# Sums and denominators of seven attention slabs by one operation of eight products, realigned through DRAM; first loads and operation order changed

## The chip, the core and the metric

The kernel runs on one core of a Trainium2 chip. A core has five engines that run side by side, each through its own list of instructions in order: PE (matrix products; its weight loads are listed apart as PEld), DVE and ACT (elementwise work and reductions on up to 128 partitions), POOL (the same, slower) and SP (which here only issues DMAs). ACT can issue DMAs too. DMAs move data between DRAM and the core's memory (SBUF); products land in PSUM, eight banks of 128 partitions x 512 FP32 values, from where DVE or ACT copy them out. Engines wait for each other by semaphores. The metric is the device time of one execution in microseconds (us), as a median over runs.

## The reference

Four blocks in a row on x (2048 tokens, 512 features): attention, gated MLP, attention, gated MLP, each on a layer-normalised copy and added to x. The attention is linear, with 32 heads of 16 features:

```python
pq = jnp.einsum("bhsd,hdf->bhsf", q, w_phi)
pk = jnp.einsum("bhsd,hdf->bhsf", k, w_phi)
phi_q = jnp.concatenate([_softmax(pq, axis=-1), _softmax(-pq, axis=-1)], axis=-1)
phi_k = jnp.concatenate([_softmax(pk, axis=-1), _softmax(-pk, axis=-1)], axis=-1)
kv = jnp.einsum("bhsf,bhsd->bhfd", phi_k, v)
z  = jnp.einsum("bhsf->bhf", phi_k)
num = jnp.einsum("bhqf,bhfd->bhqd", phi_q, kv)
den = jnp.einsum("bhqf,bhf->bhq", phi_q, z)[..., None] + 1e-6
o = num / den
```

The MLP is `h = relu(x @ W_gate) * (x @ W_up)`, `h @ W_down`, with 1376 hidden features. Both layers use the same weights.

What matters for the change: for every query and head the softmaxes of pq and -pq need two sums of exponentials (sign 0 and sign 1, 16 terms each), and den needs two more products, exponentials times z. From these four numbers the kernel makes one factor for each sign, so that it can multiply the bare exponentials instead of dividing three times: with sums Z0, Z1 and denominators D0, D1, the factor of sign s is Z(1-s) / (D0 Z1 + D1 Z0).

## The kernel before, in words

The 16 tiles of 128 tokens stand in five slabs of 2, 4, 4, 4 and 2 tiles (`SLABS`), 256 or 512 tokens each. x stays in SBUF. For each layer the program goes through these stages; the tag in brackets is the one in the code, followed by layer and slab:

- layernorm to a normalised, transposed copy (`la`, and `lg` ahead of the MLP). It is transposed either by a DMA on SP's queue (L848, for the keys in `XPOSE`) or by PE in strips of 32 (L872) with four copies. Slab 2 of layer 0 (`a02`) is done by PE.
- keys (`k`): k and v products, exponentials of both signs (L900), their sums (L906) and reciprocals, v scaled by them (L920), products into `kvsum` (L932, L942). All slabs must be through before the sums stage `su` can use `kvsum`.
- queries (`q`): products into a bank, exponentials of both signs into `expq` (L1001).
- `attend`: sums of exponentials (`z`, with the stationary block `ZO`) and denominators (`at`, with `ZD`), both at L1016. A slab has 32 + 32 small products: for each of four column strips (32 columns of the array) a quarter of the slab's tokens, so that the results lie as (quarter, head) on 128 partitions. ACT copies the sums out (`Zs`, L1050), DVE multiplies (`zm`, L1058) and adds (`zden`, L1060), ACT takes the reciprocal by Ln and Exp (L1061, L1062), DVE makes the factors `aT` (L1063).
- spreading (`sp`): the factors must reach the 16 rows of every head. Slabs 0 and 1 do that by PE (L1137) with DVE and ACT behind it; slabs 2, 3 and 4 by DRAM: two writes (L1073) and eight broadcast reads (L1077) on SP's queue into `abT` (four chunks, one for eight heads), then one product for each chunk on DVE or POOL (L1122).
- numerators (`nm`, L1089, 32 products on 16 tiles of 32 x 32), output projection (`wo`), residual (L1159).
- MLP (`gx` and `gl` for gate and up, `d` for down); slab st + 1's attention is put into the program ahead of slab st's MLP.

The order on each engine is fixed when the program is built. A planner (`Program.schedule`) walks through all operations with estimated durations and takes, at each step, the ready operation that can start first; the list `TURNS`, one number for each operation, decides among them. The table `ENG` says which engine takes an eviction, a scaling or a load. On the chip each engine then follows its list and waits where its semaphores tell it to; a wait on SP's queue holds every DMA behind it.

The plain products of all stages go through `mm` (L673); `evict` (L769 to L775) copies a bank out by DVE or ACT.

The branch that the change switches on is in the code already (L1025 to L1039), but `ZALL = ()`:

```python
if (L, st) in ZALL:
    def all_sums(e):
        for s in range(2):
            for c in range(NC):
                ins = e.matmul(zd.f32()[32 * c:32 * c + 32, 0:n], ZA[:, s, c, :], eqv(st)[:, c, s, :], start=s == 0, stop=s == 1, tile_position=(0, 32 * c))
        return ins
```

Of the kernel before, what the change touches and what calls it, by code (L numbers as in the profile page):

```python
# [12 lines left out]
P = 128  # L13
# [10 lines left out]
ENG = {'ap/a00/0': 'act',  # L24
 'ap/a01/3': 'dve',
 'ap/a02/2': 'dve',
 'ap/a02/3': 'dve',
# [3 lines left out]
 'ap/a11/0': 'act',  # L31
 'ap/a11/3': 'act',
 'ap/a12/1': 'act',
 'ap/a12/2': 'act',
 'ap/a12/3': 'act',
 'ap/a13/1': 'act',
 'ap/g01/1': 'act',
 'ap/g01/2': 'act',
 'ap/g01/3': 'act',
 'ap/g02/0': 'act',  # L40
 'ap/g03/1': 'act',
 'ap/g03/2': 'act',
 'ap/g03/3': 'act',
 'ap/g04/0': 'act',
 'ap/g04/1': 'act',
 'ap/g11/1': 'act',
 'ap/g11/3': 'act',
 'ap/g12/3': 'act',
 'ap/g13/2': 'act',
 'ap/g13/3': 'act',  # L50
 'ap/g14/0': 'act',
 'ap/g14/1': 'act',
 'em/00/01': 'dve',
 'em/01/01': 'dve',
 'em/10/01': 'dve',
 'em/10/03': 'dve',
 'em/11/03': 'dve',
 'es/02/1': 'pool',
 'es/02/2': 'pool',
 'es/02/3': 'pool',  # L60
# [3 lines left out]
 'es/04/3': 'pool',  # L64
 'es/12/1': 'pool',
# [4 lines left out]
 'es/14/0': 'pool',  # L70
 'es/14/2': 'pool',
 'fcq0': 'dve',
 'fcq2': 'dve',
 'ld/wk2': 'sp',
 'ld/x1': 'act',
 'ot/00/3': 'act',
 'ot/01/1': 'dve',
 'ot/01/3': 'dve',
 'ot/02/1': 'dve',
 'ot/02/3': 'dve',  # L80
 'ot/03/1': 'dve',
 'ot/04/2': 'dve',
 'ot/10/0': 'dve',
 'ot/10/2': 'dve',
 'ot/10/3': 'act',
 'ot/11/1': 'dve',
 'ot/12/0': 'dve',
 'ot/12/2': 'dve',
 'ot/13/3': 'dve',
 'ot/14/2': 'dve',  # L90
 'rz/0/12': 'act',
 'rz/0/13': 'act',
 'rz/0/14': 'act',
 'rz/0/4': 'act',
 'rz/0/6': 'act',
 'rz/0/9': 'act',
 'rz/1/11': 'act',
 'rz/1/12': 'act',
 'rz/1/14': 'act',
 'rz/1/15': 'act',  # L100
 'rz/1/3': 'act',
 'rz/1/4': 'act',
 'rz/1/5': 'act',
 'rz/1/8': 'act',
 'vc/0/13': 'dve',
 'vc/0/3': 'dve',
 'vc/0/6': 'dve',
 'vc/0/7': 'dve',
 'vc/1/1': 'dve',
 'vc/1/11': 'dve',  # L110
 'vc/1/12': 'dve',
 'vc/1/2': 'dve',
 'vc/1/3': 'dve',
 'vc/1/5': 'dve',
 'vc/1/6': 'dve',
 'vc/1/8': 'dve',
 'vh/0/10/1': 'dve',
 'vh/0/12/1': 'dve',
 'vh/0/13/1': 'dve',
 'vh/0/14/0': 'dve',  # L120
 'vh/0/15/0': 'dve',
 'vh/0/15/1': 'dve',
 'vh/0/6/1': 'dve',
 'vh/0/8/0': 'dve',
 'vh/0/8/1': 'dve',
 'vh/1/0/0': 'dve',
 'vh/1/1/0': 'dve',
 'vh/1/10/0': 'dve',
 'vh/1/11/0': 'dve',
 'vh/1/12/0': 'dve',  # L130
# [3 lines left out]
 'vh/1/2/0': 'dve',  # L134
# [4 lines left out]
 'vh/1/7/0': 'dve',  # L139
 'vh/1/8/0': 'dve',  # L140
 'vh/1/9/0': 'dve',
 'vh/1/9/1': 'dve',
 'xp/a02': 'pe',
# [3 lines left out]
 'yc/a00/1': 'dve',  # L147
 'yc/a01/00': 'act',
 'yc/a01/03': 'act',
 'yc/a02/02': 'act',  # L150
 'yc/a03/00': 'act',
# [20 lines left out]
 'yc/g11/03': 'act',  # L172
# [3 lines left out]
 'yc/g14/03': 'act'}  # L176
XPOSE = ('a02', 'a03', 'a04', 'a11', 'a12', 'a13', 'g01', 'g02', 'g03', 'g12', 'g13', 'g04', 'g14')
XISSUE = 1270.0
XDELAY = 215.0
BIG = 'sp'  # L180
# [3 lines left out]
ZALL = ()  # L184
TURNS = """
-28 300 427 180 240 186 0 614 40 120 554 928 1235 801 988 674 1362 1422 1115 1175 1482 1602 1662 1782 1542 1722 56 6 0 84 174 104 211 54 124 64 144 76
119 161 204 247 290 332 375 91 76 117 191 242 218 696 181 629 635 640 646 680 726 732 737 743 805 801 806 812 818 886 845 850 856 861 903 778 784 790
795 838 867 873 878 884 1009 241 357 386 424 542 570 663 668 674 680 728 299 373 405 440 252 318 560 566 571 771 980 1002 1023 1090 1306 1327 1366
1387 1141 1237 1318 1484 1477 1550 1656 959 1045 1067 1112 1219 1241 1263 1284 1189 1381 1598 1772 1429 1943 1837 1923 2201 2737 1794 1842 1848 1908
1955 1349 1355 1360 1539 1573 1653 1702 1854 1859 1895 1609 1615 1642 1647 1733 36 549 48 534 638 756 580 764 793 828 896 963 1002 934 1003 1072 970  # L190
1165 1333 1250 1284 1285 1729 1750 1799 1821 1772 2019 2062 2084 2092 1906 2287 2529 2237 2594 2700 1431 1452 1517 1659 1409 1544 1620 1680 1858 1800
2014 2187 1814 2252 2358 1474 1495 1566 1587 1865 1976 1997 2105 1685 1637 2629 2776 2808 2189 2953 2847 2329 2394 2416 2437 1707 1886 1954 2040 2535
2487 2794 2962 2140 3165 3059 2868 3304 3441 838 1243 1069 1526 1185 1533 1127 1706 1781 1848 1881 1888 1954 2023 2122 2155 2232 2462 2428 2495 2395
2643 2664 2772 2815 2600 2621 2686 2708 2870 2918 3004 3246 3310 2902 3349 3741 2729 2751 2949 2971 3100 3187 3208 3230 3069 3021 3177 3384 3324 3561
3455 3014 3036 3057 3079 3122 3144 3165 3273 3262 3129 3476 3692 3327 3906 3843 2794 2837 2928 2992 3364 3429 3450 3472 3444 3511 3584 3790 3993 3559
4137 4031 3892 4328 4505 2229 2779 1426 1874 1714 2787 1540 2772 2825 2860 3112 3317 3177 3375 3804 3285 3270 3524 3856 3397 3537 3559 3580 3602 3623
3645 3688 3710 3732 3684 3969 4095 3876 4243 4349 3839 3952 3973 4016 4038 4060 4081 4103 4066 4114 4187 4355 4162 4455 4561 4124 4146 4168 4189 4211
4232 4431 4517 4287 4239 4397 4602 4667 4619 4705 4818 3775 3818 3861 3995 3667 3731 3753 3796 4410 4506 4579 4734 4799 4295 4944 4881 4700 5235 5352
3119 3426 3492 3626 3734 3807 3983 2571 3433 3607 3780 3836 3924 4110 4254 4276 4297 4388 4582 4604 4647 4668 4554 4458 4687 4819 4884 4751 5163 5050
4409 4452 4539 4770 4474 4496 4560 4625 4836 4900 4973 5099 4686 5226 5289 5285 5412 5465 5515 5559 5525 2589 4759 4868 4998 5117 5150 5182 5215 5363  # L200
5315 3493 3504 3515 3526 4857 4901 4912 4987 5027 5075 5474 5531 5605 5662 5697 5751 5783 5821 5875 5998 6092 5939 5949 6058 6384 6456 6476 6486 6516
6550 6572 6593 6748 6812 6926 7073 6615 6636 6726 6769 6791 6868 6977 7011 7044 7121 7208 7272 7278 7284 7289 7326 6984 7025 7063 7095 7185 7191 7196
7202 7273 2127 2148 2170 2308 2358 2406 2567 3252 3385 3407 3636 4009 2459 2481 2502 2524 2632 2583 2286 2351 2373 2545 2680 2728 4801 4948 5630 5725
5773 5813 5850 5893 6232 6543 6304 6383 6340 6602 6090 6151 6147 6509 6244 6196 6443 6668 6749 6808 6797 6749 7295 7316 7338 7360 7419 6990 7033 7208
7251 7595 6925 7055 7076 7098 7148 6947 6968 7012 7229 7360 7537 7771 7713 7793 7655 7786 7479 7778 7822 7895 7941 7927 7934 8111 8093 7955 8024 8302
8429 8048 8175 7414 7597 7616 7625 7917 7947 8097 8138 8210 8278 8676 7381 7392 7477 7488 7532 7542 7586 7633 7786 7797 8117 8127 8147 8158 8168 8179
7672 8219 7422 7433 7444 7564 7575 7753 7764 7808 7403 7709 7840 7873 7895 7906 7925 7936 7847 7975 7499 7666 7687 7698 7731 7742 7829 7884 7955 7966
8010 8021 8032 8065 8223 8234 8348 8431 7510 7521 7553 7644 7655 7775 7851 8054 7676 7819 7862 8075 8086 8106 8201 8212 8300 8372 7455 7466 7605 7720
7977 7988 7999 8043 8190 8245 8256 8267 8278 8289 8343 8805 8162 8845 8321 8354 8375 8397 8551 8573 8594 8616 8927 8949 9357 9407 8300 8419 8440 8462
8646 8676 8697 8719 8971 8992 9039 9089 9587 9706 9175 9249 9735 9809 9893 9921 10033 10068 10255 13237 13259 13269 13340 14966 14988 15096 15290  # L210
13392 13441 13519 13682 15390 15624 15463 15074 15441 15873 15916 12933 13019 13062 13154 15966 16014 16107 16287 13198 16347 16410 19480 19501 19560
5052 5074 5096 5128 5219 5267 4944 5161 5381 5509 5559 5607 4879 4966 5009 5031 5123 5171 4923 5193 5338 5359 5411 5459 5733 5871 6002 6211 6363 6436
6594 6636 6751 6691 7087 7207 7327 7267 7027 6907 6967 7147 7827 7887 7389 7603 8493 8622 8633 8574 8574 9601 9688 9709 10076 10126 9753 9904 10012
10163 10259 8762 8784 8816 8838 8904 9731 9796 9817 9839 9900 10201 10319 10334 10408 8979 9053 9975 10099 10438 10473 10505 10558 10557 10621 10589
10991 10610 10864 10737 9298 9306 9487 9495 9504 9555 9563 9571 9608 9714 8638 8667 8903 8911 8919 9014 9022 9030 9067 9148 9881 9276 9422 9465 9925
10184 10271 10292 10379 9990 10429 9512 9623 9645 9666 9082 9444 9533 9580 9761 9833 8859 9190 9211 9233 9168 9255 9314 9401 9283 9467 9947 10098
10120 10228 10249 10314 10336 10400 10510 10654 10530 10552 10573 10595 9860 9882 9968 9990 10645 10717 8741 8881 9060 9103 10638 10660 10681 10703
9548 10776 10357 10444 10465 10487 10141 10422 10508 10616 10734 10836 9125 9147 9336 9379 11159 11246 11289 11375 10798 11425 9774 10033 10055 10206
10987 11051 11073 11138 10857 11188 10724 10746 10789 10832 10767 10811 10854 10875 10917 11047 12184 12205 12227 12249 12270 12317 12363 12385 12436
# [133 lines left out]
class Program:  # L353
    SYNC = 120.0
    SAME = 60.0
    DMA_ISSUE = {"sp": 600.0, "act": 560.0, "pool": 1100.0}
    DMA_LAT = 1800.0
    DMA_BW = 270.0
    SWITCH = 95.0
# [64 lines left out]
    def schedule(self):  # L424
# [6 lines left out]
        qfree = ported = 0.0  # L431
# [897 lines left out]
```

## Time and profile before

| | us |
|---|---|
| median of 3 runs | 390.58 (389.74 to 391.33) |
| the profiled execution | 390.76 |
| its span, first to last instruction | 389.0 |
| PE busy | 373.5 (96% of the span) |
| DVE, ACT, POOL busy | 275.5, 193.8, 66.6 |
| sums and denominators, 640 products at L1016 | 10.7 (sum of their busy times) |
| DMA moved | 24.33 MB, most of it in the first 30 us |

Busy time of an engine is the time in which it works on an instruction; a matmul is listed with its whole passage through the array (379 ns for 512 columns), although the next one starts 0.22 us behind it, so that the busy time of PE overlaps and says little about how dense the work is. The chain of waits goes back from the last instruction to what released each step; its pieces give the true pace of consecutive products. In the table of groups a line is one kind of instruction at one line of the code, with its count, its total and mean time, and the idle time ahead of it on its engine. The code's lines (L...) are those of the kernel before.

### The profile page before, as it was taken

The page shows a single profiled execution, that of the slowest core. Times are in us where ns is not written, and L with a number is a line of the kernel's source. Part 1 is how long each engine was busy: PE and PEld are TensorE (multiplying, and loading weights), DVE is VectorE, ACT ScalarE, POOL GpSimd, SP SyncE. Part 2 cuts the span into 40 slices and gives each one's busy share as a digit, 9 for nine tenths or more (in the row PEclk, how much of TensorE's full clock was granted, in tenths as well). Part 3 has the DMA queues.
Part 4 walks back from the last instruction along what each step waited for, and adds up shares of the span by engine and source line. Part 5 has one row for each costly group of instructions (what it writes and reads, how often), then busy time and mean ns, then how long its engine had stood idle before and what let it go on. Part 6 is the DMA issues. An engine that isn't in the chain of part 4 may idle for free.

```text
span 389.0 us, 9735 instructions
## 1 busy us (share of the span) xinstructions
PE 373.5 (96%) x4097; PEld 201.7 (52%) x4151; DVE 275.5 (71%) x561; ACT 193.8 (50%) x432; POOL 66.6 (17%) x59
## 2 busy tenths in 40 slices
PE   6999998999999999999999999999999999999996
PEld 3555455584444444454456555558444454444574
DVE  8999988885973676994359997899778234344343
ACT  4899899562360334393135659975153213212320
POOL 0168440151310000121003124003530000000000
PEclk9999999999999999999999999999999999999999
DMA  9992200224340000431000200015540201010111
GB/s 211 297 357 46 48 3 3 90 72 112 109 68 2 13 0 15 95 56 40 0 3 17 48 16 17 4 60 133 133 108 15 45 11 41 27 29 28 42 34 54
DMA packets 53067, 24.33 MB, mean 63 GB/s; under 512 B 38976, under 2 KB 52000, under 8 KB 53024
## 3 DMA queue, kind: packets, MB, share of 16 engines
q1 hardware_dynamic: 52208, 23.51, 24.2%
q8 instruction: 32, 0.52, 0.6%
q10 hardware_dynamic: 816, 0.21, 0.3%
q14 instruction: 11, 0.09, 0.1%
HBM read 12.89 MB, written 2.42 MB: 39 GB/s over the span
## 4 chain that ended last, share of the span: by engine, by line
PE 85%; ACT 4%; DMA 3%; DVE 3%; issue 2%; SPq 1%
PE pb L673 80%; DMA yG<-ytile 2%; ACT expk L900 2%; PE pb L932 2%; PE pb L1016 1%; DMA x_sb<-in_A_x_dram 1%; DVE expq L1155 1%; PE pb L1089 1%; SPq L848 1%; ACT expq L1001 1%; DVE stats L798 0%; ACT gate_sb L1211 0%; ACT ytile L840 0%; DVE oT L771 0%; PE pb L872 0%
## 5 line engine op out<-in xcount | busy, mean ns | idle before, releaser
L673 PE MATMUL pb<-yG,Wg 128*128 128x512 bf16 (+1 forms) x394 | 100.3, 336 | 1.1 <-DMA yG<-ytile 0.7
L673 PE MATMUL pb<-yG,Wu 128*128 128x512 bf16 (+1 forms) x393 | 98.6, 336 | 0.6 <-issue 0.3
L1211 ACT ACTIVATE gate_sb<-pb 128x512 bf16<-128x512 f32 x80 | 47.1, 596 | 104.3 <-PE pb L673 81.5
L673 PE MATMUL pb<-Wd,hT 128*128 128x512 bf16 (+2 forms) x352 | 97.1, 373 | 1.5 <-issue 0.9
L1213 DVE TENSOR_TENSOR hT<-gate_sb,pb 128x512 bf16<-128x512 bf16 x80 | 53.7, 683 | 53.9 <-PE pb L673 39.2
L920 POOL TENSOR_TENSOR vhat<-vsb,rZk 128x544 bf16<-128x544 bf16 x38 | 41.1, 1101 | 140.9 <-DVE x_sb L1159 48.1
L1159 DVE TENSOR_TENSOR x_sb<-x_sb,pb 128x512 bf16<-128x512 bf16 x59 | 39.4, 679 | 29.3 <-PE pb L673 28.9
L673 PEld LDWEIGHTS pb<-yG,Wg 128*128 128x128 bf16 x400 | 39.0, 98 | 31.2 <-issue 1.0
L673 PEld LDWEIGHTS pb<-yG,Wu 128*128 128x128 bf16 x400 | 38.9, 98 | 30.4 <-DVE hT L1213 0.2
L673 PEld LDWEIGHTS pb<-Wd,hT 128*128 128x128 bf16 (+1 forms) x363 | 35.0, 98 | 35.6 <-issue 2.0
L900 ACT ACTIVATE expk<-pb 128x512 bf16<-128x512 f32 x64 | 35.5, 603 | 21.7 <-PE pb L673 18.2
L906 DVE TENSOR_REDUCE Zk<-expk 128x64 f32<-128x1024 bf16 x32 | 38.4, 1204 | 3.8 <-ACT expk L900 3.8
L798 DVE BATCH_NORM_STATS2 stats<-x_sb 128x6 f32<-128x512 bf16 x60 | 39.8, 682 | 0.6 <-DMA x_sb<-in_A_x_dram 0.3
L1122 POOL TENSOR_TENSOR expq<-expq,abT 128x1024 bf16<-128x1024 bf16 (+1 forms) x14 | 24.8, 1777 | 79.8 <-DMA abT<-spread 24.5
L673 PE MATMUL pb<-Wkp,yA 128*128 128x512 bf16 x124 | 37.3, 390 | 0.8 <-issue 0.5
L673 PE MATMUL pb<-wv,yA 128*128 128x512 bf16 x122 | 35.0, 379 | 0.4 <-issue 0.2
L673 PE MATMUL pb<-wo_sb,oT 128*128 128x512 bf16 x121 | 34.7, 379 | 0.6 <-DVE stats L798 0.2
L1001 ACT ACTIVATE expq<-pb 128x512 bf16<-128x512 f32 x64 | 34.9, 628 | 0.6 <-PE pb L673 0.4
L673 PE MATMUL pb<-yA,Wqp 128*128 128x512 bf16 (+1 forms) x147 | 32.0, 333 | 2.0 <-issue 1.0
L840 ACT ACTIVATE ytile<-x_sb,nmr,rstd 128x512 bf16<-128x512 bf16 x33 | 25.7, 814 | 3.2 <-DVE nmr L832 3.2
L673 PE MATMUL pb<-Wl,yG 128*128 128x192 bf16 x128 | 21.6, 246 | 0.7 <-DMA yG<-ytile 0.6
L673 PEld LDWEIGHTS pb<-yA,Wqp 128*128 128x128 bf16 x160 | 14.3, 98 | 11.4 <-issue 0.2
(87 smaller groups left out, 323.8 us busy)
## 6 DMA issues: line engine op xcount, KB each, us to landing
abT<-spread SPq DMA_DIRECT2D x32, 128.0 KB
out_dram<-x_sb SPq DMA_DIRECT2D x15, 128.0 KB, 1.7
x_sb<-in_A_x_dram SPq DMA_DIRECT2D x3, 512.0 KB
Wg<-in_B_W_gate_dram SPq DMA_DIRECT2D x1, 1280.0 KB, 7.4
Wu<-in_B_W_up_dram SPq DMA_DIRECT2D x1, 1280.0 KB, 10.1
Wd<-in_B_W_down_dram SPq DMA_DIRECT2D x1, 1280.0 KB, 12.7
abT<-spread SPq DMA_DIRECT2D x16, 64.0 KB
wv<-in_A_wqkv_dram SPq DMA_DIRECT2D x1, 512.0 KB
```

The lines of the kernel that those rows point to most:

```text
L673: op("pe", lambda e: e.matmul(view(ps), lhsT, rhs, start=start, stop=stop), reads=reads, writes=[ps], occ=max(25.0, 0.4167 * n + 2.6), lat ...
L798: op("dve", lambda e: e.bn_stats(stats[:, t, :], src()), reads=[res], writes=[R("st", t)], occ=580, lat=680, name=f"bn{t}")
L840: op("act", (lambda t, yb: lambda e: e.activation(ytile[:, yb, :], x_sb[:, t, :], ACT.Identity, bias=nmr[:, t, :], scale=rstd[:, t, :]))(t ...
L900: op("act", (lambda i, s, pk: lambda e: e.activation(expk[:, i, s, :], full(pk), ACT.Exp, scale=1.0 - 2.0 * s))(i, s, pk), reads=[pk], wri ...
L906: op("dve", (lambda i, zb: lambda e: e.tensor_reduce(Zk[:, zb, :], expk[:, i, :, :].rearrange("p s (h f) -> p (s h) f", f=16), AX.X, ALU.a ...
L920: op(eng, (lambda i, s, vb, rz: lambda e: e.tensor_tensor(vhat[:, i, s, :, :], vsb[:, vb, :, :], rZk[:, rz, s * 32:(s + 1) * 32].unsqueeze ...
L932: ins = e.matmul(ps.f32()[32 * i:32 * i + 32, g * 34:g * 34 + 34], expk[:, tiles[j], sg, f0:f0 + 32], vhat[:, tiles[j], sg, 8 * c + 2 * i: ...
L1001: op("act", (lambda c0, s, ps: lambda e: e.activation(eqv(st)[:, c0:c0 + per, s, :], ps.f32()[:, 0:per * n].rearrange("p (c n) -> p c n", ...
L1122: op(eng, lambda e: e.tensor_tensor(part, part, abT[:, c].rearrange("p (s n) -> p s n", s=2)[:, :, 0:n], ALU.mult), reads=Re + [R("abT", c ...
L1159: op("dve", lambda e: e.tensor_tensor(x_sb[:, t, :], x_sb[:, t, :], full(ps), ALU.add), reads=[R("x", t), ps], writes=[R("x", t)], occ=597 ...
L1211: op("act", (lambda gb, pg, k: lambda e: e.activation(gate_sb[:, gb, 0:k], pg.f32()[:, 0:k], ACT.Relu))(gb, pg, k), reads=[pg], writes=[R( ...
L1213: op("dve", (lambda gb, hb, pu, k: lambda e: e.tensor_tensor(hT[:, hb, 0:k], gate_sb[:, gb, 0:k], pu.f32()[:, 0:k], ALU.mult))(gb, hb, pu, k),
```

## The change

For seven of the ten slabs (slabs 2, 3, 4 of layer 0 and 1, 2, 3, 4 of layer 1) the sums and denominators are made in one operation of eight products: for each sign and each chunk of eight heads one product with all the slab's tokens (512 or 256 columns), whose stationary block `ZA` holds, for each head, four columns: two for the sums, two for the denominators. The four chunks lie on the four column strips. The result lies as (head, which of the four numbers) on the partitions and token along the bank, which is not the order that the rest needs. So the bank is copied to SBUF (into chunk 0 of `abT`, as FP32), written to a DRAM scratch (256 KB for 512 tokens) and read back as (quarter, head) on the partitions with the four numbers side by side in `Zs`. `zm` then reads both factors from SBUF.

```diff
-ZALL = ()
+ZALL = ((0, 2), (0, 3), (0, 4), (1, 1), (1, 2), (1, 3), (1, 4))
+LATE = 300.0
+TRUNC = 0
...
-    DMA_ISSUE = {"sp": 600.0, "act": 560.0, "pool": 1100.0}
-    DMA_LAT = 1800.0
-    DMA_BW = 270.0
+    DMA_ISSUE = {"sp": 630.0, "act": 500.0, "pool": 1100.0}
+    DMA_LAT = 2000.0
+    DMA_BW = 360.0
...
                 evict(ENG.get(f"za/{L}{st}", "act"), lambda: Zn, lambda: zd.f32()[:, 0:n], n, zd, [], R_Zn, f"zac{st}")
-                dma("sp", lambda e: e.dma_start(zscr[:, 0:n], Zn), reads=R_Zn, writes=[R("zscr")], nbytes=512 * n, name=f"zao{st}")
+                dma("sp", lambda e: e.dma_start(zscr[:, 0:n], Zn), reads=R_Zn, writes=[R("zscr")], nbytes=512 * n, name=f"zao{st}", delay=LATE)
                 zk = Zs[:].rearrange("p g n -> p (g n)")[:, 0:4 * w].rearrange("p (k w) -> p k w", w=w)
-                dma("sp", lambda e: e.dma_start(zk, zscr[:, 0:n].rearrange("(h k) (q w) -> q h k w", k=4, w=w)), reads=[R("zscr")], writes=[R("Zs", 0), R("Zs", 1)], nbytes=512 * n, name=f"zai{st}")
+                dma("sp", lambda e: e.dma_start(zk, zscr[:, 0:n].rearrange("(h k) (q w) -> q h k w", k=4, w=w)), reads=[R("zscr")], writes=[R("Zs", 0), R("Zs", 1)], nbytes=512 * n, name=f"zai{st}", delay=LATE)
...
+        def fill(fn, writes, n, name):
+            eng = ENG.get(f"ms/{name}", "dve")
+            op(eng, fn, writes=writes, occ=60 + 0.85 * n if eng == "dve" else 200 + 1.05 * n, name=name)
...
-        op("dve", lambda e: e.tensor_tensor(BD.rearrange("p c (h f) -> p c h f", f=16),
+        bd = ENG.get("ms/BD", "dve")
+        op(bd, lambda e: e.tensor_tensor(BD.rearrange("p c (h f) -> p c h f", f=16),
```

`LATE` and the constants of `Program` are estimates that the planner uses; no instruction waits for them. `TRUNC = 0` leaves the program whole.

The rest of the diff is in `ENG` and `TURNS`:

- `TURNS` has new numbers for all operations, so the order on every engine is another one.
- `xp/a02: pe` is gone: slab 2 of layer 0 is transposed by four DMAs on SP's queue, which stand behind the loads of Wu and (three of them) Wd.
- The loads of x0, wk3, x8 and x12 go from SP's queue to ACT's, which already had x1 and wphi.
- The block `BD` and the first fills of `ZO`, `kvsum` (layer 0) and its small constants go from DVE to POOL.
- Evictions, scalings, layernorm applications and reciprocals change between DVE, ACT and POOL in many places: among them two more evictions of slab 1's spread in layer 1 to ACT, and four of the seven new evictions (`za/...`) to DVE, three to ACT.

The lists of instructions change so: PE has 3695 products instead of 4151 (392 fewer at the sums and denominators, 64 fewer in strips), SP issues 174 DMAs instead of 160 (seven writes and seven reads of the scratch and four transposes more, four loads fewer), ACT seven instead of three. In layer 1 the first 33 gate and up products of slab 0's MLP stand ahead of slab 1's numerators.

## The prediction

> **What bounds the kernel now.** I read the page's busy shares first, then busy time by stage (cut at the places where the work changes character), then the chain of waits, the groups by shape, and the DMA issues. Columns of the stage view: stretch, length, then busy time (and instructions) of PE, PEld, DVE, ACT, POOL.
>
> ```profile
> PE 373.5 (96%) x4097; PEld 201.7 (52%) x4151; DVE 275.5 (71%) x561; ACT 193.8 (50%) x432; POOL 66.6 (17%) x59
> ```
>
> ```profile
> 10.00:57.20 47.20, 45.55 (x834) 23.93 (x840) 45.81 (x86) 43.33 (x98) 24.78 (x23) 1.00 0.55 153
> 57.20:69.50 12.30, 11.01 (x354) 6.49 (x357) 10.18 (x26) 12.10 (x32) 0.00 (x0) 1.00 0.01 3
> 69.50:238.00 168.50, 165.46 (x1457) 87.93 (x1476) 124.67 (x243) 75.82 (x170) 27.11 (x21) 1.00 0.20 44
> 238.00:259.50 21.50, 20.39 (x638) 12.13 (x645) 18.00 (x43) 20.64 (x54) 1.10 (x1) 1.00 0.03 7
> 259.50:389.00 129.50, 124.66 (x790) 67.87 (x801) 68.52 (x136) 36.80 (x74) 12.88 (x7) 1.00 0.21 56
> ```
>
> Five stages are to be seen. Until 57.2 (keys and values of layer 0) PE, DVE and ACT are all over 90% busy: no single one decides. From 57.2 to 69.5 (sums, spreading of slabs 0 and 1 of layer 0) ACT has 12.10 of 12.30 and PE has 1.3 us free. From 69.5 on PE sets the pace: it is idle 3.0 us in 168.5. At 238 to 259.5 (the same step of layer 1) ACT again has 20.64 of 21.50, PE 20.39. After that PE again, up to a tail of some 4 us. So PE time removed after 69.5 counts in full, time removed between 57.2 and 69.5 counts for nothing, and time removed between 238 and 259.5 counts if other PE work can take the place while ACT catches up.
>
> **The eight-product operation.** The chain shows what the 64 products of a slab cost today, and what a column-tiled operation with 512 columns costs. (Start, length, what.)
>
> ```profile
> 60.34 0.63 PE pb L1016 x32
> ...
> 67.11 0.35 PE pb L1016 x32
> ...
> 74.20 0.56 PE pb L1016 x32
> ...
> 99.77 10.74 PE pb L673 x49
> ...
> 112.67 0.58 PE pb L1089 x32
> ...
> 251.05 0.37 PE pb L1089 x32
> ...
> 253.51 0.16 issue
> ```
>
> A slab of 512 tokens has two operations of 32 products (sums, then denominators): 2 x 0.56 = 1.12. The new one has eight products of 512 columns on four column strips, that is two waves of 512 columns; the numerator operation (L1089, 32 products on 16 tiles) is also two waves of 512 columns and takes 0.58. The difference is 0.54, and one change into and out of tiled mode less (0.16 of "issue" behind such an operation): 0.70. A slab of 256: 2 x 0.35 against 0.37, and 0.16: 0.49. The seven slabs are five of 512 and two of 256: 5 x 0.70 + 2 x 0.49 = 4.5 us of PE time. Bounds: not below 0.45 per large slab (no saving on the mode change, 0.67 as for the slower L1089), nor above 0.83 (two at 0.63 against 0.43, the pace of two plain 512-column products at 10.74 / 49 = 0.219).
>
> Where it counts. Slab 2 of layer 0 and the first half of slab 4 lie in 57.2 to 69.5: nothing. Of layer 0, the second half of slab 4 and both halves of slab 3 lie behind 69.5; the changed order puts their new operations ahead of slab 1's numerators, in the stretch where PE has 1.3 us free, so 0.35 + 2 x 0.56 + 0.16 = 1.6 leaves the PE-bound part. Layer 1 has 3 x 0.70 + 0.49 = 2.6 in the ACT-bound stretch. There the change begins slab 0's GLU products between slab 1's spreading products (33 matmuls of 256 columns, some 3.7 us, ahead of slab 1's numerators), work that needs ACT for about a third of PE's time (596 ns for 16 of them, 1.8 us). ACT's own load there hardly changes: four Zs copies go (3 x 0.41 + 0.31), one 512-column eviction comes (0.60) and two evictions of slab 1's spread move to it (2 x 0.63). I take 2.0 of the 2.6; bounds 0 and 2.6.
>
> **The way through DRAM.** Each of the seven slabs gets an eviction of the whole bank (0.68 on DVE, 0.60 on ACT, in place of Zs at 0.41), a DMA of 256 KB to DRAM and one back, and the old multiply and add from SBUF. SP issues 14 DMAs more (0.6 each by its plain issues). The trace has no such round trip; the nearest rows, from issue to landing:
>
> ```profile
> out_dram<-x_sb SPq DMA_DIRECT2D x15, 128.0 KB, 1.7
> ...
> wo_sb<-in_A_wo_dram SPq DMA_DIRECT2D x4, 128.0 KB, 4.3
> ```
>
> Lower end 1.7 (half the bytes, quiet), upper end 4.3 (short strided pieces in a crowded queue). I take 2.1: 1.7 and 128 KB more at the 350 KB/us that the page shows at its fullest (slice of 357 GB/s), since these stretches move 3 to 7 GB/s. The chain from the new operation to the factors aT is then 0.68 + 2.1 + 2.1 + 1.9 (zm to aT, 244.91 to 246.83 today) + some 0.5 for hand-overs = 7.3 us. Between the new operation of layer 1's slab 1 and its spread products the changed order has 30 matmuls of 512 columns, 16 of 256 and three tiled ones: 30 x 0.219 + 16 x 0.113 + 1.3 = 9.7. Margin 2.4. For slab 2 of layer 0 the round trip lands while DVE still multiplies slabs 0 and 1, until about 69 as today, so DVE's order holds zm, not DRAM: aT at 71.2, its two writes landed at 73.2, the eighth load issued at 73.2 + 7 x 0.61, landed 2.7 later, one product of 0.7: 80.9. PE comes to the numerators at 60.3 + 22.9 of work + 1.3 idle as today = 84.5. Margin 3.6.
>
> The Trainium skill ("DMA: Bandwidth & Descriptors", Anatomy of one DMA) speaks against this part: about 2 us of a DMA are fixed, mostly the receipt of the last write, with HBM the slowest target, and its fit (made on GpSimd's queue) is 2.0 us plus bytes over 436 KB/us: an estimate of 2.6 here. The trace's 1.7 for a store lies below that. By the page a round trip would be 1.0 us longer, and the forecast 388.3.
>
> **What is queued behind.** The bank is evicted into chunk 0 of abT, so slab 3's eviction must wait for slab 2's product of that chunk, and slab 4's for slab 3's; until then one or two of eight PSUM banks are held, and the eviction stands in ACT's or DVE's order. In layer 1 the SP queue has, in this order: loads of slab 2's abT, slab 3's write and read, and then the four transposes that slab 1's GLU needs. Slab 3's write waits for a POOL product (2.12), its read waits for the write (2.1), and only then do the transposes start, of which today's last one takes this:
>
> ```profile
> 273.21 2.51 SPq L848 DMA_TRANSPOSE yG<-ytile  x2
> ...
> 274.45 4.33 DMA yG<-ytile
> ```
>
> From the new operation of slab 3: some 2.5 until slab 2's aT, 2.0 for its two writes, 3.3 until chunk 0 has landed (today POOL starts at 76.51, 2.7 after the fourth load's issue), 2.1 POOL, 0.6 eviction, 2.1 write, 0.6 issue of the read, 3 x 1.26 ahead of the last transpose: 17.0, and it lands 3.7 (86.99 to 90.70) to 4.3 later, at 20.7 to 21.3. PE has 73 matmuls of 256, 51 of 512 and two numerator operations, 20.6 us, before the GLU's first product. With the held banks I take 0.8 us of new waiting, bounds 0 and 3. Layer 0's SP order leaves 0.5 to 1 us there, where today PE waits 0.75 for yG at 90.2; I count nothing.
>
> **The start and the moved operations.** x0, wk3, x8 and x12 go to ACT's queue (4 x 0.41 to 0.46, in the 5 us that ACT is idle in the first ten); BD and three fills go to POOL, idle there. Slab 2's tiles are transposed by four DMAs (1.26 each on SP, behind Wu and Wd) instead of 64 small products (0.59) and four copies (0.41 each on DVE, 0.6 on ACT). These can land as late as 33 to 34, because the weights keep the queues full until about 30; today's products of that slab start at 28.6. The order puts 32 query products ahead of them as cover; without it PE would stand 4 us. Summed by the durations of the old rows, the keys stage has DVE 1.0 us less, ACT 2.5 more (1.8 of it the four issues), POOL 1.9 less. I take 0.5 us off the end of the stage; bounds 2.0 off and 3 on. The rest of the reassignments (layer 0: ACT 4.8 less, DVE 5.5 more, POOL 3.3 less; layer 1: ACT 5.8 more, DVE 5.8 less, POOL 6.5 more) lie in stretches where ACT is 28 to 45% and DVE 53 to 74% busy: hidden behind PE; if one came late, it would show as a wait of its own length.
>
> **The sum.** -1.6 - 2.0 - 0.5 + 0.8 = -3.3. The profiled execution took 390.76, its span 389.0 and 1.76 around it; it stands 0.18 above the median of the three runs, 390.58. So span 385.7, and 387.3 on the median's scale.
>
> **The rivals.**
> - The gain is eaten by ACT: 57.2 to 69.5 and 238 to 259.5 last as long as ACT needs, layer 1 gives nothing, and the start gives nothing. For it: ACT's 96 and 98%, the extra 1.3 us of evictions. Against: the GLU work that fills in. 390.58 - 1.6 + 0.8 = 389.8: no change.
> - Slower: the round trips take 4.3 a transfer. It decides from 3.3 on, when the margin of 2.4 is gone. Then slab 1's spread in layer 1 is 2.0 late, slab 2's round trip and slab 3's write hold SP so that the transposes for slab 1's GLU come 4.4 + 2.2 later, of which 3.6 remain after the first wait and 1.0 of slack; in layer 0 the last transpose for slab 1's GLU stands behind slab 3's write and read, with two transposes between: 4.3 - 2 x 1.26 = 1.8 late, 1.0 beyond the slack. 6.6, less 0.8 already counted: 387.3 + 5.8 = 393.1. For it: an in-order SP queue, 512 B pieces, a read that must wait for its write. Against: the 1.7 of the stores.
> - The change doesn't do what it says: the eight products don't overlap on the four strips. Eight x 0.219 = 1.75 against 1.12 today, -0.16 saved: the large ones 0.47 slower, the small ones (8 x 0.113 against 0.70) 0.04: 2.4 slower in place of 3.6 faster: 393.3. Against: 32 products of 128 columns in 0.56 are 17.5 ns each, a third of 128 columns' time.
> - The start gains its full 2.0 and nothing waits: 387.3 - 1.5 - 0.8 = 385.0.
>
> **How the numbers follow.** About 0.5% (2 us) is what a measurement of this kernel can tell from no change. Chances: forecast 0.46 (its own range 385.2 to 388.6), eaten by ACT 0.22, late round trips 0.20, no overlap 0.03, fuller gain 0.09. The range reaches from the fuller gain over the late round trips: 383.8 to 393.2. Faster: forecast and fuller gain, 0.55; same: 0.22; slower: 0.23.
>
> **What would show it.** L1016 falls from 640 to 192 products, and the new line has 56 with about 0.58 a group of eight at 512 columns (1.7 would be the third rival). Writes and reads of the new scratch land within 2.1 (over 3.3: the second). PE's idle time before slab 1's spread in layer 1 and before its GLU stays under 1 us. The keys stage ends at 56.5 to 57.2; the stretch from slab 1's numerators in layer 0 to the end is 3 to 4 us shorter than today's 319.5. The forecast is wrong if that stretch is not shorter, or if the keys stage ends after 59.

## The result and the profile after

| | us |
|---|---|
| changed kernel, median of 4 runs | 407.48 (403.19 to 408.68) |
| kernel before beside it, 4 runs | 390.16 (389.12 to 391.33) |
| ratio | 1.0426, 95% interval 1.0383 to 1.0469: slower |
| the profiled execution and its span | 403.19, 401.5 |

387.3 was forecast, and the range ended at 393.2. The page and the stages of the changed kernel, cut at the same events as before (last product into `kvsum`, numerators of slab 1, sums of layer 1's slab 0, the last sums); columns as in the stage view above, with the granted clock, the share of the 16 DMA engines and GB/s at the end:

```profile
span 401.5 us, 8918 instructions
...
PE 379.3 (94%) x3695; PEld 196.8 (49%) x3695; DVE 274.0 (68%) x561; ACT 196.8 (49%) x438; POOL 67.2 (17%) x62
```

```profile
10.00:63.65 53.65, 49.75 (x823) 25.59 (x823) 47.61 (x89) 45.65 (x109) 20.51 (x19) 0.89 0.65 153
63.65:75.45 11.80, 10.62 (x253) 5.10 (x252) 10.06 (x25) 11.34 (x28) 0.00 (x0) 1.00 0.11 36
75.45:252.00 176.55, 170.86 (x1516) 88.71 (x1515) 128.33 (x250) 78.24 (x175) 27.20 (x22) 0.99 0.22 48
252.00:271.30 19.30, 17.33 (x270) 8.57 (x269) 12.32 (x33) 15.71 (x37) 0.00 (x0) 1.00 0.18 57
271.30:401.50 130.20, 126.14 (x819) 66.94 (x819) 69.90 (x144) 41.96 (x84) 17.03 (x9) 1.00 0.25 63
```

The work per engine is almost what it was (DVE 274.0, ACT 196.8; PE's 379.3 hold stretches at half clock); the time is lost to standing still. The keys stage ends at 63.7 in place of 57.2, with PE idle 3.9 of 53.7 us (before 1.7 of 47.2). The middle stage, which was to get shorter, has PE idle 5.7 us in 176.6 (before 3.0 in 168.5; some 2.5 us of the rest are work that has moved into it, 128 small products into `kvsum` and six query products); in the spreading stage of layer 1 PE is idle 2.0 and ACT, 96% busy before, is at 81%: it is no longer what bounds there. The chain of waits says on what the time goes (start, length, what):

```profile
3.69 12.03 DMA wv<-in_A_wqkv_dram
...
63.72 0.31 PE pb L971 x32
...
66.98 0.55 PE pb L1068 x8
...
72.20 5.64 DMA Zs<-sums_scr
77.84 0.02 issue
77.86 0.44 DVE zm L1094
...
96.67 5.65 DMA yG<-ytile
...
257.53 5.66 DMA Zs<-sums_scr
...
265.32 5.62 DMA Zs<-sums_scr
```

For the eight-product operation of a slab of 256 tokens, two lines of the timeline of PE (start, time, ...):

```profile
74.14 0.40 PE L1068 MATMUL pb<-expq,ZA 128*32 128x256 bf16 x8 [0.50 <-ACT expq L1040]
74.48 1.04 PE L706 MATMUL pb<-wo_sb,oT 128*128 128x512 bf16 x4
```

Four things are to be seen. The eight-product operation (L1068) takes 0.55 for a slab of 512; for one of 256 the next product starts 0.34 behind its start. Three read-backs stand on the chain with 5.6 us each, and DVE's `zm` starts the moment they land. The transposes for slab 1's MLP in layer 0, issued at 96.67 right behind a read-back, take 5.65 too (before 3.71). And the chain begins with the load of `wv`, 12 us from its issue. So there are two separate losses: the reads from the scratch and the start.

### The profile page after: what moved, and what is told of

The parts are those of the page before. It is cut to its first block, busy times and chain, and to the rows that moved or that the text cites. A ratio compares the mean times of both kernels' runs of the same rounds, so it can differ in the third digit from the quotient of the medians.

```text
span 401.5 us, 8918 instructions
## 1 busy us (share of the span) xinstructions
PE 379.3 (94%) x3695; PEld 196.8 (49%) x3695; DVE 274.0 (68%) x561; ACT 196.8 (49%) x438; POOL 67.2 (17%) x62
## 4 chain that ended last, share of the span: by engine, by line
PE 84%; DMA 10%; DVE 3%; SPq 1%; ACT 1%; issue 0%
PE pb L706 80%; DMA Zs<-sums_scr 4%; DMA wv<-in_A_wqkv_dram 3%; DMA yG<-ytile 3%; PE pb L971 2%; DVE expq L1194 1%; PE pb L1128 1%; PE pb L1055 1%; DVE zm L1094 0%; SPq L735 0%; SPq L887 0%; PE pb L1068 0%; ACT oT L813 0%; DVE ytile L882 0%; SPq L729 0%
## 5 line engine op out<-in xcount | busy, mean ns | idle before, releaser
L706 PE MATMUL pb<-yG,Wu 128*128 128x512 bf16 (+1 forms) x400 | 95.0, 336 | 4.5 <-DMA yG<-ytile 3.3
L706 PE MATMUL pb<-Wd,hT 128*128 128x512 bf16 (+2 forms) x363 | 95.4, 374 | 0.0
L706 PE MATMUL pb<-yG,Wg 128*128 128x512 bf16 (+1 forms) x400 | 94.9, 337 | 0.0
L959 POOL TENSOR_TENSOR vhat<-vsb,rZk 128x544 bf16<-128x544 bf16 x36 | 39.0, 1104 | 125.3 <-DVE vhat L959 43.6
L945 DVE TENSOR_REDUCE Zk<-expk 128x64 f32<-128x1024 bf16 x32 | 38.3, 1207 | 4.3 <-ACT expk L939 4.3
L706 PE MATMUL pb<-wv,yA 128*128 128x512 bf16 x128 | 38.1, 395 | 2.0 <-DMA wv<-in_A_wqkv_dram 2.0
L706 PE MATMUL pb<-wo_sb,oT 128*128 128x512 bf16 x128 | 36.3, 391 | 2.1 <-DVE oT L810 1.8
L706 PE MATMUL pb<-yA,Wqp 128*128 128x512 bf16 (+1 forms) x160 | 34.4, 338 | 0.0
L879 ACT ACTIVATE ytile<-x_sb,nmr,rstd 128x512 bf16<-128x512 bf16 x31 | 24.1, 807 | 2.4 <-DVE nmr L871 2.4
L1218 ACT ACTIVATE gate_sb<-pb 128x192 bf16<-128x192 f32 x16 | 5.3, 332 | 33.0 <-PE pb L706 32.8
L706 PEld LDWEIGHTS pb<-wo_sb,oT 128*128 128x128 bf16 x128 | 12.4, 99 | 17.4 <-DVE oT L810 2.5
```

What stands on the lines that cost most here:

```text
L706: op("pe", lambda e: e.matmul(view(ps), lhsT, rhs, start=start, stop=stop), reads=reads, writes=[ps], occ=max(25.0, 0.4167 * n + 2.6), lat ...
L879: op("act", (lambda t, yb: lambda e: e.activation(ytile[:, yb, :], x_sb[:, t, :], ACT.Identity, bias=nmr[:, t, :], scale=rstd[:, t, :]))(t ...
L945: op("dve", (lambda i, zb: lambda e: e.tensor_reduce(Zk[:, zb, :], expk[:, i, :, :].rearrange("p s (h f) -> p (s h) f", f=16), AX.X, ALU.a ...
L959: op(eng, (lambda i, s, vb, rz: lambda e: e.tensor_tensor(vhat[:, i, s, :, :], vsb[:, vb, :, :], rZk[:, rz, s * 32:(s + 1) * 32].unsqueeze ...
```

## The experiments

Times are medians in us, each beside the kernel before on the same chip. The last three columns are stretches of the profiled execution: up to the start of the last product into `kvsum` of layer 0, from there to the same point of layer 1, and from there to the start of PE's last product.

| run | time | before | ratio (95%) | to keys, layer 0 | to keys, layer 1 | rest |
|---|---|---|---|---|---|---|
| kernel before | | | | 57.4 | 184.8 | 143.1 |
| changed kernel | 407.48 | 390.16 | 1.0426 (1.0383, 1.0469) | 63.9 | 187.6 | 146.7 |
| wide read-back | 393.69 | 389.04 | 1.0106 (1.0071, 1.0141) | 65.4 | 180.2 | 143.6 |
| loads back | 400.39 | 389.04 | 1.0293 (1.0260, 1.0326) | 60.2 | 188.1 | 146.4 |
| both | 389.76 | 389.04 | 1.0026 (1.0013, 1.0040) | 60.8 | 180.3 | 143.7 |
| no eight products | 398.26 | 389.04 | 1.0238 (1.0203, 1.0274) | 63.9 | 181.1 | 148.4 |
| spliced | 386.45 | 389.66 | 0.9912 (0.9887, 0.9936) | 56.5 | 180.8 | 143.7 |
| before, new loads | 395.42 | 389.66 | 1.0140 (1.0115, 1.0164) | 63.6 | 184.8 | 143.0 |
| slab 2 by PE | 396.69 | 389.66 | 1.0174 (1.0149, 1.0198) | 65.7 | 182.5 | 143.5 |
| before, x8 and x12 early | 392.62 | 389.96 | 1.0066 (1.0049, 1.0084) | 60.1 | 184.4 | 142.7 |
| spliced, slab 2 by DMA | 396.13 | 389.96 | 1.0134 (1.0094, 1.0175) | 65.8 | 181.5 | 144.1 |
| four reads | 403.60 | 390.25 | 1.0345 (1.0304, 1.0387) | 65.9 | 185.5 | 147.0 |

The changed order leaves some 1.9 us of PE work behind the second mark that lies ahead of it in the order before (six query products, 6 x 0.219, and the sums of slabs 0 and 1 of layer 1, 0.2 + 0.4); whoever compares the last two columns with the first row has to move that much.

### The read-back over 16 engines

```diff
-        zscr = nc.dram_tensor("sums_scr", (128, 512), FP32, kind="Internal").ap()
+        zflat = nc.dram_tensor("sums_scr", (128 * 512,), FP32, kind="Internal").ap()
...
-e.dma_start(zscr[:, 0:n], Zn)
+e.dma_start(zflat[0:P * n].rearrange("(q p w) -> p q w", q=4, w=w), Zn.rearrange("p (q w) -> p q w", w=w))
...
-e.dma_start(zk, zscr[:, 0:n].rearrange("(h k) (q w) -> q h k w", k=4, w=w))
+e.dma_start(zk, zflat[0:P * n].rearrange("(p k w) -> p k w", k=4, w=w))
```

> The changed kernel with another layout of the DRAM scratch: the write puts the sums down as (quarter, head, number, token) in pieces of 512 B, so that the read-back has 128 rows of 2 KB in place of four quarters of 128 pieces; same bytes, same order on every engine. Theory 'four engines': the read-back of the changed kernel lands after 5.6 us because its outermost count is 4 and it runs on a quarter of the 16 DMA engines (DMA share 0.27 to 0.30 while it runs, 86 GB/s). Then it lands here within 2.5 us, at a DMA share over 0.6, the waits at 72 to 78, 96 to 102 and 257 to 271 shrink by about 3 us each, and the time falls from 407.5 by 7 to 10, to 397 to 400. Rival 'pieces or target': a read from DRAM right behind its write, or pieces of 512 B, are slow by themselves; then the write gets slower or the read stays over 4, and the time stays within 3 of 407.5.

393.69: 13.8 below the changed kernel, more than either theory gave. First the read itself. Two rows of the DMA view of the changed kernel, 66 to 79 us in 40 equal slices: busy share of the 16 DMA engines in tenths, and GB/s.

```profile
DMA  0000000005980000000000001222222251000000
GB/s 0 0 0 0 0 0 0 0 0 139 353 315 0 0 13 6 25 6 0 0 0 0 0 17 49 76 87 87 79 88 87 87 131 50 21 0 0 0 0 0
```

The same view of the wide version, 68.5 to 76 us, and its rows of issues (count, KB, median from issue to landing):

```profile
DMA  0000000000044999820000000000000007068971
GB/s 0 0 0 0 0 0 0 0 0 0 0 87 150 279 284 281 257 60 0 5 11 8 14 22 22 5 0 0 0 0 0 0 0 87 11 208 339 382 295 66
```

```profile
sums_scr<-abT SPq DMA_DIRECT2D x5, 256.0 KB, 2.6
Zs<-sums_scr SPq DMA_DIRECT2D x5, 256.0 KB, 2.6
```

In the changed kernel the write moves nearly all its bytes in three slices at up to 353 GB/s; its last packets come one at a time until 71.6, and the read is issued at 72.20. The read of the same 256 KB creeps along at 87 GB/s for 3 us, with two to three tenths of the DMA engines busy. The trace's packets say that few engines work, and not that all of them work slowly: during the read mostly four or five packets are under way at once, during the bulk of the write mostly 15 or 16. Shared among four engines, 87 GB/s are some 22 for each. With 128 rows in place of four quarters it runs at up to 382 GB/s and lands in 2.6. The write, now in pieces of 512 B, goes from 2.1 to 2.6. What that does to DVE shows in the group of `zm` (large slabs; busy, mean ns, idle time before it and its cause), the changed kernel first, the wide one second:

```profile
L1094 DVE TENSOR_TENSOR zm<-Zs 128x256 f32<-128x256 f32 x5 | 2.1, 425 | 10.1 <-DMA Zs<-sums_scr 10.1
```

```profile
L1101 DVE TENSOR_TENSOR zm<-Zs 128x256 f32<-128x256 f32 x5 | 2.1, 421 | 1.0 <-DMA Zs<-sums_scr 1.0
```

The second and third stretch get shorter by 7.4 and 3.1 us, the first is 1.5 longer. The rest of the 13.8 lies in the comparison: the profiled execution of the changed kernel is the fastest of its four, 4.3 below their median. The granted clock alone is not the cause of the slow start: in the changed kernel it was 0.50 from 10 to 20 us, in this run 1.00 there, and the keys stage ended later still, at 65.4. It has a part in the changed kernel's profiled execution, though: the first ten products of the keys stage take 4.24 us there from 15.77 on, and 2.19 at 0.219 each, so some 2 us are the clock's.

### The read in four parts

That run changed the write and the size of the pieces too, so the number of engines was tested alone: same layout, same pieces, one DMA for each quarter.

```diff
-e.dma_start(zk, zscr[:, 0:n].rearrange("(h k) (q w) -> q h k w", k=4, w=w))
+for q in range(4):
+    e.dma_start(zk[32 * q:32 * q + 32], zscr[:, q * w:(q + 1) * w].rearrange("(h k) w -> h k w", k=4))
```

> The changed kernel with each read-back cut into four DMAs, one for a quarter, 32 rows each; the DRAM layout, the pieces of 512 B, the bytes and the order of every engine stay, SP issues 21 DMAs more. Theory 'four engines': each quarter now has 32 as its outermost count and runs on all 16 DMA engines, so it lands about 2 us after its own issue, and the last of the four some 4 after the first one's issue (three issues of 0.6 more), in place of 5.6; the transfers show 200 GB/s or more in place of 87, and the time falls by 2 to 7, to 400 to 405. Rival 'pieces': 512 B pieces read from DRAM are slow on any number of engines; then the whole read-back still takes 5.6 or more at about 87 GB/s and the time is 407 or more.

403.60, 3.9 below the median of the changed kernel, whose fastest run, the profiled one, took 403.19; so the time alone says little. From its chain of waits, in layer 0:

```profile
74.19 0.54 SPq L1090
...
75.41 0.60 SPq L1090
...
76.05 2.53 DMA Zs<-sums_scr
```

Each quarter lands 2.4 after its issue (median), the last one 4.5 after the first was issued at 74.04, against 5.64 in one piece. DVE's `zm` of the five large slabs now waits 6.5 us for `Zs` in place of 10.1, that of the two small ones 4.3 in place of 1.8. So pieces of 512 B are not what is slow: a packet of 512 B takes 27 ns (median) in both runs, but up to 16 are under way at once here. The GB/s expected were not reached (at most 137): 64 KB every 0.6 us are 109 GB/s, so the issues now set the pace, and SP is held that long. Of the two cures tried, the one DMA with many rows is the better.

### The loads, back and alone

```diff
+SP_LOADS = [0, 8, 9, 3, 4, 1, 2, 10, 7, 15, 13, 11, 14, 18, 19, 12, 16, 17, 20, 24, 21, 22, 25, 23]
+ACT_LOADS = [6, 5]
...
+        for eng, loads in (("sp", SP_LOADS), ("act", ACT_LOADS)):
+            for i, k in enumerate(loads):
+                self.ops[k].eng, self.ops[k].start = eng, 10.0 * i
```

(The numbers are those of the loads in the program: 0 is x0, 4 wk3, 7 wv, 10 x8, 11 x12; this is the order of the kernel before.)

> The changed kernel with the loads of x0, wk3, x8 and x12 back on SP's queue and all loads in the order of the kernel before; every other instruction keeps its engine and its place. Theory 'start': wv lands at 15.7 in place of about 10.5 because x8 and x12 (1 MB) run on ACT's queue beside it, PE stands until it is there and runs at half clock for 10 us. Then the first keys are ready at 11 to 11.5, the last products into kvsum come at 57 to 58.5 in place of 63.7, and the time falls by 5.5 to 7, to 400.5 to 402. Rival 'evictions and transposes': the moved operations (BD and fills on POOL, slab 2 transposed by DMA, the other evictions) make the keys stage longer; then the first keys come early and the end of the stage stays after 61, and the time falls by under 3.

> Both edits of the two runs before at once. If the two theories hold, and nothing else is wrong with the prediction, the gains add: 407.5 - 6.3 - 8.5 = 392.7, and with the waits that share a cause, 389 to 393; PE's savings of 3.6 (1.6 and 2.0 in the prediction) then show against the kernel before as 387 to 390. If a third cost is left (the other evictions, held banks, the order), it stays above 394.

The same edit on the kernel before, with the lists of the changed kernel, and then with x8 and x12 alone moved to ACT:

```diff
+SP_LOADS = [8, 3, 9, 1, 7, 2, 12, 14, 13, 16, 15, 18, 20, 23, 17, 25, 24, 21, 19, 22]
+ACT_LOADS = [6, 5, 0, 4, 10, 11]
```

```diff
+SP_LOADS = [0, 8, 9, 3, 4, 1, 2, 7, 15, 13, 14, 18, 19, 12, 16, 17, 20, 24, 21, 22, 25, 23]
+ACT_LOADS = [6, 5, 10, 11]
```

> The kernel before with nothing changed but the loads: x0, wk3, x8 and x12 on ACT's queue and the loads on SP's in the order of the changed kernel. Theory 'start': wv lands 3 to 5 us later than the 10.5 of the kernel before, the last product into kvsum comes 4 to 6.5 later than 57.2, and the time is 389.0 + 4 to 7 = 393 to 396. Rival: the loads hurt only together with the changed order of the keys stage; then the time stays within 1.5 of 389.0.

> The kernel before with only the loads of x8 and x12 (512 KB each) put on ACT's queue, behind wphi; SP's loads keep the order of the kernel before without these two, and every other instruction its place. Theory 'megabyte ahead': these two loads, issued at about 2.5 instead of 5.9 and 9.9, take the DMA engines ahead of wk0, wk1 (transposed on SP) and wv, about 1 MB at some 300 KB/us, 3.5 us; then the first keys come 3 to 6 later than 11.0, and the time is 389.4 + 3 to 6 = 392.4 to 395.4, most of the 5.8 that the whole new order of loads costs. Rival: the order on SP (wv after one transpose in place of after two and x8) or x0 and wk3 make it; then the time stays within 1.5 of 389.4.

Loads back gave 7.1, both edits together 17.7 (389.76, inside the 389 to 393 expected); on top of the wide read-back the loads are worth 3.9. With loads back the keys stage ended at 60.2, though, not at the expected 57 to 58.5: something else at the start is late too (below). The kernel before loses 5.8 by the new order of loads alone, all of it before its keys stage ends (63.6; the other stretches are unchanged). Of that, x8 and x12 make 2.7, less than the 3 to 6 expected; the rest comes with x0, wk3 and the order on SP, which was not split further. The mechanism shows on SP's queue. First two lines of the timeline of the changed kernel, then one line each of the chain of waits with x8 and x12 early and with all new loads:

```profile
3.69 0.96 SPq L747 DMA_DIRECT2D wv<-in_A_wqkv_dram  x1
4.71 10.78 SPq L735 DMA_TRANSPOSE hT<-in_A_wqkv_dram  x4
```

```profile
3.26 9.12 DMA hT<-in_A_wqkv_dram
```

```profile
4.32 11.89 DMA hT<-in_A_wqkv_dram
```

Four transposing loads hold SP for 10.8 us; in the kernel before two take 2.60 and two more 2.77. A megabyte of x that the kernel before uses from 13 us on goes out on the second queue at 3 to 4 us and is moved beside wk and wv, which PE waits for. In the changed kernel PE's listed waits up to its last product into `kvsum` add up to 9.2 us, in the kernel before to 5.2, and none of the 9.2 lies behind 15.8 us. The 4.0 more and the some 2 us of half clock are nearly all of the 6.4 by which its keys stage ends late.

### Without the eight products

```diff
-ZALL = ((0, 2), (0, 3), (0, 4), (1, 1), (1, 2), (1, 3), (1, 4))
+ZALL = ()
```

(The old operations take the places of the new ones in `TURNS`.)

> The changed kernel without the eight-product operation: the seven slabs make sums and denominators by 64 small products as before, with no way through DRAM; first loads, engines and the order of the rest as changed. By the two theories the start's 6.5 us is all that is left: 396 to 398. If the new order and reassignment cost on their own, it lies above 399; if they gain, below 395.

398.26, just above the first range and below the second: the new order neither gains nor costs much on its own. Beside it the operation with the wide read-back is worth 4.6 us (398.26 to 393.69), and with the read-back as changed it costs 9.2 (407.48). The rest stretch is the longest of all, 148.4; that an order made for the short operation is bad for the long one would explain it, but was not tested.

### The rest of the keys stage

With both edits the keys stage still ended 3.4 us late. The chain of that run:

```profile
30.62 0.06 ACT rstd L879
30.68 4.12 DMA yA<-ytile
34.80 0.14 issue
```

This looked like the DMA transposes of slab 2 (`yA<-ytile`). The spliced version takes the whole keys stage (orders, engines, loads) from the kernel before and all behind it from the changed kernel with the wide read-back; the planner is held to these lists:

```diff
+        line = {e: sorted((o for o in self.ops if o.eng == e), key=lambda o: -o.prio) for e in ENGINES}
...
+                        if o is not line[e][-1]:
+                            continue
```

> The keys stage of layer 0 (everything that the kernel before starts up to its last product into kvsum) in the order, on the engines and with the loads of the kernel before; everything behind it in the order and on the engines of the changed kernel, with the eight-product operation and the wide read-back. Theory: the start is all that the version with loads back and wide read-back still loses, 60.6 against 57.2 at the last product into kvsum; then that product is at 57 to 57.7 here, the rest lasts 324 as there, and the time is 389.8 - 3.4 = 386.4 (385.5 to 387.5), faster than the kernel before (389.0) by 1.5 to 3.5, close to what was predicted for the change. Rival: the rest had more time to prepare behind the late start and now waits for ACT and DVE; then the gain shows at 57 and is given back by 75, and the time stays within 1 of 389.0.

386.45, where 386.4 was expected, and faster than the kernel before: the rest needs nothing that the changed start prepares. Its busy times, and its spreading stage of layer 1:

```profile
PE 375.1 (98%) x3759; PEld 196.6 (51%) x3759; DVE 274.9 (72%) x569; ACT 196.8 (51%) x432; POOL 69.8 (18%) x61
```

```profile
238.00:255.30 17.30, 16.59 (x271) 8.66 (x270) 13.37 (x36) 16.10 (x41) 0.00 (x0) 1.00 0.22 63
```

Engine times are again the same, but PE is at 98% in place of 94. In the spreading stage ACT is 93% busy and PE 96%: GLU products do fill in beside ACT. Then slab 2's transposes, both ways: added to the table `ENG` of the version with both edits, and taken out of that of the spliced one.

```diff
+ 'xp/a02': 'pe',
```

```diff
- 'xp/a02': 'pe',
```

> The version with loads back and wide read-back, and slab 2 of layer 0 transposed by 64 small products as in the kernel before, in place of four DMAs (the planner orders anew around it). Theory: the DMA transposes land at 34.8 and the products of slab 2's keys start 4 us later than before (32.4 against 28.6), and that makes the 3.4 us by which its keys stage still ends late; then the last product into kvsum comes at 57.5 to 59 and the time falls from 389.8 to 387 to 388.5. Rival: the other moved evictions, scalings and fills make it; then it stays at 60 to 61.5 and 389 to 390.5.

> The version of the spliced run (keys stage as before, the rest as changed, wide read-back) with slab 2 of layer 0 transposed by four DMAs on SP's queue, right ahead of slab 3's, in place of 64 small products and four copies; every other instruction keeps its place, so PE has no cover put ahead of that slab's keys. Theory of the prediction: the DMAs land at 30 to 34 because the weights fill the queues until about 30; the products of slab 2's keys, at 27.5 in the spliced run, then wait 3 to 6 us, DVE and ACT are relieved by 2, and the time rises from 386.5 to 388.5 to 391. Rival: they land within 3 of their issue and cost nothing, 385.5 to 386.5.

The first fell outside both ranges: 396.69, 6.9 slower than without the edit. Its chain:

```profile
27.50 0.70 ACT ytile L893
...
30.60 0.49 ACT expq L1054
31.10 0.05 issue
31.14 0.65 PE pb L925 x64
```

In the changed order slab 2's layernorm ends at 28.2 (24.5 in the kernel before), while ACT has made seven copies of the folded weights by 32 us in place of four; PE transposes at 31.1 and gains nothing. The planner also ordered the rest anew, and the chain runs through DVE from 70.9 to 75.5, which has nothing to do with the question: this run settles nothing about the DMAs. The second one does: it leaves every other instruction in its place, and costs 9.7 (386.45 to 396.13), more than either theory gave. Its chain and what PE waited for from 10 to 60 us (us in total, times, longest):

```profile
25.91 8.05 DMA yA<-ytile
33.97 0.14 issue
34.10 4.61 PE pb L689 x11
```

```profile
PE pb L689 <- DMA yA<-ytile: 8.1, 2, 6.8
```

The first wait for the transposes ends at 34.0, 8 us after the first issue, and PE stands 6.8 us at once. Behind that the clock was granted at 0.50 from 31.5 to 38.3 us, and the eleven products of the last line took 4.61 us where 11 x 0.219 is 2.4. Waits of 8.1 and these 2.2, less the 0.6 of the small products left out, come to the 9.7.

This is the price without cover. The changed kernel and the version with both edits have 32 query products ahead of slab 2's keys, and there PE hardly waits for the transposes. From PE's waits between 5 and 57 us in the version with both edits:

```profile
PE pb L719 <- ACT rstd L879: 1.5, 1, 1.5
...
PE pb L719 <- DMA yA<-ytile: 0.2, 1, 0.2
```

The 1.5 us end at 32.42 with the first products of slab 2's keys, and the profile puts them down to ACT; the transposes themselves cost 0.2. In the changed kernel no wait for them is listed at all. Up to the last product into `kvsum` PE's waits add up to 8.7 us with both edits and to 5.2 in the kernel before, which is the 3.4: some 2 of it lie ahead of 17.3 us (transposed weights, wv, the first copies of them) and 1.7 at slab 2's keys. Which of the operations moved to other engines make these waits stays open.

## Why the prediction was wrong

- **The eight products: right.** 0.58 and 0.37 were taken, 0.55 and 0.34 were measured, and the third rival (no overlap, 1.75) is out.
- **The way through DRAM: the step that failed.** It said "I take 2.1" for each transfer, "1.7 and 128 KB more at the 350 KB/us that the page shows". That holds for the write in the median (2.1), though SP waited 3.5 us for the first one to land. The read took 5.6, above the upper bound of 4.3 too. It was priced by its bytes from rows that all have 128 or 32 partitions outermost; that its own outermost count is four stood in the diff (`q h k w`) and was not weighed. With it the chain of 7.3 became 10.8, and the margins of 2.4 and 3.6 were used up. (By these margins a round trip 1.0 longer would not have shown, so the 388.3 does not follow from the prediction's own sum.) "DVE's order holds zm, not DRAM" was wrong for layer 0's slab 2: DVE waited for DRAM until 77.84. What stands behind such a read on SP's queue paid as well: PE waited 3.6 us for transposes in layer 0 (0.6 with the wide read-back). This is the second rival's mechanism with a worse price: it had 5.8 for 4.3 a transfer; between 10.6 (400.39 to 389.76, loads back) and 13.8 were measured.
- **The start: the other step that failed.** "I take 0.5 us off the end of the stage; bounds 2.0 off and 3 on" became 6.4 on. The four loads were costed as four issues on an idle ACT. What they do, with the new order of the loads on SP's queue, to the weights that PE needs first was not costed at all; it is 5.8 us in the kernel before. For slab 2's transposes the prediction was right: the landing at "33 to 34" (34.8 and 34.0 were measured), and the 32 query products as cover (PE waits 0.2 us for them with both edits, 8.1 in the run without cover, where "4 us" was said).
- **The gain: right in size.** The spliced version has the change without these two steps, and its 386.45 is 3.2 below the kernel before, against 3.3 forecast; of the 3.3 the start was to give 0.5, which this version does not have, so 2.8 is the like sum. By stretches and with the 1.9 us moved: layer 0 -4.0 + 1.9 = -2.1 (forecast -1.6), layer 1 +0.6 - 1.9 = -1.3 (forecast -2.0 + 0.8 = -1.2). The 0.8 of new waits is not to be seen, as PE's waits from 237 us to the end are 0.7 in this version (before, from 238 us, 1.9), so layer 1 agrees in its net and not in its two terms. Its start is 0.9 shorter although the instructions there are those of before; that part is taken as scatter, and so the agreement of the sum is closer than its parts deserve.
- **Eaten by ACT: not seen.** In the changed kernel ACT waits too (81%); in the spliced version it is at 93% and layer 1 still gains what was forecast.

The balance: 17.7 for loads and read-back together (407.48 to 389.76), 3.3 for the rest of the keys stage (to 386.45), less 3.2 of gain: 17.8, where 17.3 is to be explained. The terms are differences of successive runs, so the sum closes by itself but for the scatter of the kernel before, which moved by 1.1 between the groups of runs.

## What to carry to other kernels

Price a DMA by its access pattern before its bytes: look at the outermost count on both sides, and if it is small, lay out the DRAM side so that the partitions come first. A load moved to an idle queue is not free: two loads issued early cost 2.7 us here, so ask what a load now runs ahead of. Where a new round trip makes a chain longer than its cover, every in-order queue behind it pays as well, so test the chain's margin with a transfer at twice the price.

## What was unexpected of the hardware

- A read of 256 KB with four as its outermost count kept a fifth to a quarter of the DMA engines busy at 87 GB/s and landed in 5.6 us; with 128 rows outermost it ran at up to 382 GB/s and landed in 2.6; in four parts of 32 rows each part landed in 2.4. The Trainium skill says so ("DMA: Bandwidth & Descriptors", Why a DMA increments its semaphore by 16 and not by 1): the number of engines is the largest up to 16 that divides the slowest dimension on both sides. By that rule the read has four engines, and the traces agree: mostly four or five packets at once during the read, mostly 15 or 16 during the bulk of the write with its 128 rows.
- Transposing DMAs held SP's queue for long while loads were under way beside them: four took 10.78 us at the start of the changed kernel, with x8 and x12 on the other queue, where two take 2.60 in the kernel before. A high load of the DMA engines does not explain it, as from 4 to 6 us they move 342 GB/s in the kernel before and 265 in the changed one; the reason stays open. In the spliced version with slab 2 by DMA the wait for transposes issued from 25.91 on ended 8.05 later, behind the weights (355 to 384 GB/s from 20 to 30 us).
- Two loads of 512 KB on the other queue cost the kernel before 2.7 us though they were due anyway: only their time of issue changed.
